# A drain on GpSimd behind each two-source operation of an attention, FFN and expert kernel

## Chip, cores and metric

One core of one Trainium2 chip runs the whole program in one launch. The metric is the device time of one execution in microseconds; the kernel before takes 838.08 us (median of 3 runs, 837.47 to 841.38).

## What is computed

The reference, cut to its three stages (all float32; B 4, H 8, S 576, head 64, model width 512, 8 experts):

```
proj = x @ w_phi; proj -= max(abs(proj)); phi = [exp(proj), exp(-proj)]      # of q and of k
attn = (phi(q) @ (phi(k).T @ v)) / (phi(q) @ sum(phi(k)) + 1e-6)
u    = x + (x.T @ U @ V).T                # x: the attention output, 512 wide
y    = u + relu(u @ w_ch1) @ w_ch2        # hidden width 2048
e    = argmax(y @ w_gate), or the token before's where sigmoid(y @ w_local) >= 0.5
out  = softmax(y @ w_gate)[e] * (relu(y @ w1[e]) @ w2[e])
```

## The kernel before

TensorE multiplies float32 as sums of rounded parts: every operand is split into a high part (rounded to the matmul's float32 form) and a low part (the rest), and each product takes three matmuls (`three`, L973 to L975, and `mm2`, L1075 to L1077). Products of the hidden layer go through a seven-product scheme on 2x2 blocks, so sums and differences of blocks have to be made ahead of the matmuls. All of this preparation is elementwise work:

- ScalarE copies a tile into its high part (L342, L514).
- VectorE or GpSimd subtracts it to get the low part (`both`, called in `w_end`, L336 on VectorE and L67 on GpSimd; `x_end`, L517).
- VectorE or GpSimd makes the sums and differences of blocks (`sums`, L336 and L67; `add` in `x_make`, L541).
- `narrow` (L77 to L90) turns 64-bit weights into 32-bit ones in six VectorE steps and a last addition on GpSimd (L67).
- In the expert stage GpSimd scales the finished output rows (`mm2`, L1095; the last two are VectorE's).

`in_halves` (L67) issues a 512-wide operation on GpSimd as two instructions of 256 columns.

The program has an attention stage (0 to about 228 us), four FFN units of four batches (items 0 to 15) and eight expert items (16 to 23), each of some 180 matmuls. The recording itself decides the order: `gate` and `either` hold a running estimate of when each engine will be free and give a preparation step to VectorE or GpSimd when it fits beside TensorE. The engines then run their instructions in that fixed order and wait on semaphores.

Evictions of matmul results read PSUM and at most one SBUF tensor: `u`, `y` and sums in PSUM (L946), `hlo` (L948). They stand in VectorE's queue behind the preparation steps. From item 12 on, `route` (L1110 to L1207) picks the expert of a batch with many tiny VectorE steps (128x5 and 128x40), among them `r_sm` plus 1e-9 (L1161), the sum of the softmax; GpSimd's queue then issues two small transfers (L1192 and L1193). GpSimd's queue also issues the reloads of activations `x` from DRAM (L596) in the FFN units.

Of the kernel before, what the change touches and what calls it, by code (L numbers as in the profile page):

```python
# [12 lines left out]
ALU = mybir.AluOpType  # L13
# [9 lines left out]
CH = 288  # L23
# [14 lines left out]
def model(ctx, tc, kq, vx, wphi, ident, up, vp, wff, wg, wmoe1, wmoe2, rconst, outT):  # L38
    nc = tc.nc
# [12 lines left out]
    def f32(ap):  # L52
        return ap.bitcast(F32)
# [7 lines left out]
    rows = [tmp_p.tile([128, S], F32, name=f"row{n}") for n in range(NROW)]  # L61
    rawfree = [raw_p.tile([128, 1024], U32, name=f"raw{n}") for n in range(2)]

    def in_halves(eng, dst, a, b, n, op):

        for sl in (slice(0, n // 2), slice(n // 2, n)):
            eng.tensor_tensor(out=dst[:, sl], in0=a[:, sl], in1=b[:, sl], op=op)  # L67

    def narrow(dst, raw, p, n, a=None, fine=False):

# [84 lines left out]
    def cost(eng, n):  # L155
        return {"DVE": (0.075 + n / 960) * 1.15, "ACT": 0.17 + n / 1330, "POOL": 0.05 + n / 340}[eng]
# [12 lines left out]
    def gate(eng, dur, *keys):  # L169

        if not late:
            yield "step"
        while late and not force[0]:
            at = max([free[eng]] + [touched.get(id(k), 0.0) for k in keys])
            if at + (0.0 if eng == "POOL" else dur) <= free["PE"] + SLACK[eng][at_step[0]]:
                break
            yield "wait"
        emitted[0] += 1
        force[0] = False
        if late:  # L180
            book(eng, dur, *keys)

    def either(eng, n, *keys):

        if not late:
            yield "step"
            emitted[0] += 1
            return eng
        while True:
            best = None  # L190
            for e, name, bias in ((nc.gpsimd, "POOL", 0.0), (nc.vector, "DVE", BIAS)):
                dur = cost(name, n)
                at = max([free[name]] + [touched.get(id(k), 0.0) for k in keys])
                ok = at + (0.0 if name == "POOL" else dur) <= free["PE"] + SLACK[name][at_step[0]]
                if (ok or force[0]) and (best is None or at + dur + bias < best[0]):
                    best = (at + dur + bias, e, name, dur)
            if best is not None:
                break
            yield "wait"
        emitted[0] += 1  # L200
        force[0] = False
        book(best[2], best[3], *keys)
        return best[1]
# [46 lines left out]
    def later(on, issue):  # L250

        if late:
            waiting.append((touched.get(id(on), 0.0), issue))
        else:
            issue()
# [8 lines left out]
    def take(free_):  # L264

        while not free_:
            yield "blocked"
        return free_.pop(0)
# [240 lines left out]
    def x_end(key, s, r, eng, own=None, then=None):  # L509

        x = xo[key][s] = yield from take(xfree)
        keys = (x,) if own is None else (x, own)
        yield from gate("ACT", cost("ACT", 2 * CH), *keys)
        nc.scalar.copy(out=x[:, 0], in_=r)  # L514
        for k in range(2):
            use = yield from either(eng, CH, *keys)
            use.tensor_tensor(out=x[:, 1, k], in0=r[:, k], in1=f32(x[:, 0, k]), op=ALU.subtract)  # L517
        if key in xd and s in XS:
            later(x, lambda: nc.sync.dma_start(out=f32(xd[key][XS.index(s)]), in_=f32(x)))
        xdone.add((key, s))  # L520
        if then is not None:
            then()

    def as_x(r):
        return r.rearrange("p (k t) -> p k t", k=2)

    def x_make(key, due=0, keep=True, plain=False, adds=nc.gpsimd, lows=nc.gpsimd):

        b = key[1]
        xo[key] = {}  # L530
        part = {f"B{k + 1}{t + 1}": y[:, 2 * k:2 * k + 2, b * S + t * CH:b * S + (t + 1) * CH] for k in range(2) for t in range(2)}
        if keep:
            xd[key] = dram.tile([7, 128, 2, 2, CH], F32R, name=f"xd{b}")

        def add(a, c, of_=None):
            r = yield from take(rows)
            x = as_x(r)
            keys = (r,) if of_ is None else (r, of_)
            for k in range(2):
                use = yield from either(adds, CH, *keys)  # L540
                use.tensor_tensor(out=x[:, k], in0=a[:, k], in1=c[:, k], op=ALU.subtract)  # L541
            return r

        def own(s):
            if late:
                spawn("x", due, x_end(key, s, part[s], lows))
            else:
                yield from x_end(key, s, part[s], lows)

        def made(s, r, last_=True):  # L550

            def then():
                if last_:
                    rows.append(r)

            if late:
                spawn("x", due, x_end(key, s, as_x(r), lows, r, then))
            else:
                yield from x_end(key, s, as_x(r), lows)
                if plain:  # L560
                    x_drop(key, s)
                    xdone.add((key, s))
                then()

        for s in ("B11", "B21", "B12", "B22") if plain else ("B11",):
            yield from own(s)
        t1 = yield from add(part["B12"], part["B11"])
        t2 = yield from add(part["B22"], as_x(t1), t1)
        yield from made("T2", t2, False)
        yield from made("T1", t1)  # L570
        while late and len([t for t in threads if t[2] == "x"]) > 2:
            yield "wait"
        t3 = yield from add(part["B22"], part["B12"])
        yield from made("T3", t3)
        while late and len([t for t in threads if t[2] == "x"]) > 2:
            yield "wait"
        t4 = yield from add(as_x(t2), part["B21"], t2)
        while (key, "T2") not in xdone:
            yield "wait"
        rows.append(t2)  # L580
        yield from made("T4", t4)
        if plain:
            xdone.difference_update([(key, s) for s in XS if s[0] == "T"])
        else:
            yield from own("B21")
            yield from own("B22")
# [320 lines left out]
    scale = {}  # L907
# [15 lines left out]
    def then(i):  # L923

        if i < 3:
            return x_make(("f", 3), 3, adds=nc.vector) if i == 1 else None
        to = i + 2 if i < 15 else i + 3
        if to < n and not held(i):
            key = x_key(to)
            return x_make(key, to, keep=False, adds=nc.vector) if key[0] == "m" else x_load(key)  # L930
        return None
# [130 lines left out]
    def mm2(i, t, d):  # L1062

        u, b = items[i]
        t0 = b * S + t * CH
        ps, m = bank()
        free["PE"] = max(free["PE"], ps_at[m])
        for k, f in enumerate((2, 3, 0, 1)):
            hhi, hlo = hh[t, f]
            w = need_w(u, f"V{f}")  # L1070
            free["PE"] = max(free["PE"], touched.get(id(w), 0.0))
            free["PE"] = max(free["PE"], hat[t, f])
            wh = w[:, 0, d * 128:(d + 1) * 128]
            wl = w[:, 1, d * 128:(d + 1) * 128]
            nc.tensor.matmul(ps, lhsT=wh, rhs=hhi, start=(k == 0), stop=False)  # L1075
            nc.tensor.matmul(ps, lhsT=wl, rhs=hhi, start=False, stop=False)  # L1076
            nc.tensor.matmul(ps, lhsT=wh, rhs=hlo, start=False, stop=(k == 3))  # L1077
            free["PE"] += 3 * MM
            touched[id(w)] = free["PE"]
        at = free["PE"] + SYNC  # L1080
        if last[u] == i and t == 1 and d == 3:
            for s in VS:
                wfree.append(u.w.pop(s))
        dst = y[:, d, t0:t0 + CH]
        yield

        if u.kind == "moe" and u.g == 0:
            ps_at[m] = act(lambda: nc.scalar.copy(out=dst, in_=ps), CH, at)
            return
        ps_at[m] = dve(CH, at, out=dst, in0=ps, in1=dst, op=ALU.add)  # L1090
        if u.kind == "moe":
            eng = nc.vector if i + 1 == n and t == 1 and d > 1 else nc.gpsimd
            free[of(eng)] = max(free[of(eng)], ps_at[m])
            book(of(eng), cost(of(eng), CH))
            eng.tensor_tensor(out=dst, in0=dst, in1=scale[u.b][:, t * CH:(t + 1) * CH], op=ALU.mult)  # L1095
            outs.append((outT[d * 128:(d + 1) * 128, t0:t0 + CH], dst))
            if t == 1 and d == 3:
                rows.append(scale[u.b])
            if i + 1 == n:
                store(0)  # L1100
# [255 lines left out]
    with tc.For_i(0, nl):  # L1356
# [34 lines left out]
        with tc.For_i(0, FT2) as j:  # L1391
# [3 lines left out]
            for c in range(2):  # L1395
                sl = slice(c * CH, (c + 1) * CH)
# [10 lines left out]
        dst = y[:, :, bass.ds(bv * S, S)]  # L1407
# [81 lines left out]
```

## Time and profile before

| | |
|---|---|
| median of the runs | 838.08 us |
| the profiled execution | 836.82 us, span 835.0 us |
| TensorE matmul busy | 772.0 us, 92% |
| VectorE busy | 616.4 us, 74% |
| GpSimd busy | 390.0 us, 47% |
| ScalarE busy | 330.3 us, 40% |
| mean granted TensorE clock | 0.965 |

An instruction's duration runs from its start to its end and holds any time that it spends blocked inside the engine; "idle before" is time in which the engine had nothing running. A GpSimd instruction that follows another without a pause starts some hundredths of a microsecond before the end of the one ahead.

### The profile page before, as it was taken

Reading aid. Unit: us, or ns where it says so; the run is one execution under the profiler, and the core shown is the slowest. Engines: PE = TensorE matmul, PEld = TensorE weight load, DVE = VectorE, ACT = ScalarE, POOL = GpSimd, SP = SyncE. Lnnn points to the kernel's source line nnn. Section 1 sums busy time; section 2 is a strip of 40 time slices with the busy share of each in tenths; the row PEclk is TensorE's granted clock in tenths of the full one; section 3 lists DMA queues with packets and bytes.
Section 4 is the critical chain, followed back from the end, with each engine's and each line's share of the span. In section 5 each row is a group of like instructions: output and inputs, shape, how many; then the busy total and the mean of one; then the engine's idle time right before and its main releaser. Section 6 shows DMA issues by size and latency. Waiting matters only on the chain.

```text
span 835.0 us, 20754 instructions
## 1 busy us (share of the span) xinstructions
PE 772.0 (92%) x8364; PEld 748.9 (90%) x8364; DVE 616.4 (74%) x1234; ACT 330.3 (40%) x788; POOL 390.0 (47%) x519
## 2 busy tenths in 40 slices
PE   8999899988799999999999999996959949989996
PEld 6898798987699999999999999996958949989996
DVE  7898788868896566866878654569787996975743
ACT  5766677742441312122121310241626426445440
POOL 1123463545770326323562331255656866677652
PEclk9999999998999999999999999998979979999998
DMA  6444454435871056310762046403232243242511
GB/s 188 142 142 146 165 189 171 159 145 200 294 301 42 2 189 198 137 51 28 248 224 63 14 130 205 177 2 106 83 107 79 67 126 91 75 127 92 165 46 59
DMA packets 45506, 108.01 MB, mean 129 GB/s; under 512 B 5408, under 2 KB 18848, under 8 KB 45408
## 3 DMA queue, kind: packets, MB, share of 16 engines
q1 hardware_dynamic: 35648, 78.29, 27.5%
q0 software_dynamic: 6304, 24.92, 9.2%
q10 hardware_dynamic: 3456, 3.46, 1.2%
q8 instruction: 66, 1.08, 0.5%
q14 instruction: 32, 0.26, 0.1%
HBM read 77.67 MB, written 28.98 MB: 128 GB/s over the span
## 4 chain that ended last, share of the span: by engine, by line
PE 59%; DVE 16%; issue 4%; POOL 2%; ACT 2%; DMA 1%; SPq 0%; ACTq 0%; DVEq 0%; POOLq 0%
PE psf L1075 10%; PE psf L1077 10%; PE psf L1076 10%; PE psf L973 9%; PE psf L974 9%; PE psf L975 9%; DVE r_sm L1161 2%; DVE x L517 1%; DVE w L336 1%; DVE y L946 1%; DVE row L541 1%; DVE row L85 1%; DVE row L80 1%; DVE pg L698 1%; PE num L761 1%
## 5 line engine op out<-in xcount | busy, mean ns | idle before, releaser
L973 PE MATMUL psf<-x,w 128*128 128x288 f32 x676 | 204.5, 302 | 35.2 <-DVE u L946 35.2
L1075 PE MATMUL psf<-hhi,w 128*128 128x288 f32 x768 | 229.4, 299 | 1.0 <-DVE hlo L948 1.0
L1076 PE MATMUL psf<-hhi,w 128*128 128x288 f32 x768 | 227.4, 296 | 0.0
L1077 PE MATMUL psf<-hlo,w 128*128 128x288 f32 x768 | 226.6, 295 | 0.0
L975 PE MATMUL psf<-x,w 128*128 128x288 f32 x676 | 203.7, 301 | 2.1 <-DVE w L336 1.9
L974 PE MATMUL psf<-x,w 128*128 128x288 f32 x676 | 204.2, 302 | 0.0
L973 PEld LDWEIGHTS psf<-x,w 128*128 128x128 f32 x676 | 131.8, 195 | 36.9 <-DVE u L946 36.9
L1075 PEld LDWEIGHTS psf<-hhi,w 128*128 128x128 f32 x768 | 144.9, 189 | 3.4 <-DVE hlo L948 1.5
L1077 PEld LDWEIGHTS psf<-hlo,w 128*128 128x128 f32 x768 | 145.2, 189 | 0.0
L1076 PEld LDWEIGHTS psf<-hhi,w 128*128 128x128 f32 x768 | 145.0, 189 | 0.0
L67 POOL TENSOR_TENSOR row<-row,row 128x256 f32<-128x256 f32 x94 | 68.9, 756 | 150.0 <-DVE row L90 145.5
L975 PEld LDWEIGHTS psf<-x,w 128*128 128x128 f32 x676 | 131.7, 195 | 2.6 <-DVE w L336 2.1
L962 ACT ACTIVATE hhi<-psf 128x288 fp32r<-128x288 f32 x192 | 68.6, 419 | 164.2 <-DVE psf L946 158.8
L974 PEld LDWEIGHTS psf<-x,w 128*128 128x128 f32 x676 | 131.8, 195 | 0.0
L946 DVE TENSOR_TENSOR y<-psf,y 128x288 f32<-128x288 f32 x160 | 72.1, 452 | 60.4 <-PE psf L1077 59.3
L67 POOL TENSOR_TENSOR w<-row,w 128x256 fp32r<-128x256 f32 x98 | 75.7, 799 | 77.2 <-ACT w L342 62.3
L948 DVE SCALAR_TENSOR_TENSOR hlo<-psf,hhi 128x288 fp32r<-128x288 f32 x192 | 77.3, 451 | 28.6 <-ACT hhi L962 28.6
L946 DVE TENSOR_TENSOR u<-psf,p 128x288 f32<-128x288 f32 x92 | 40.8, 452 | 37.2 <-PE psf L975 36.9
L1027 ACT COPY p<-psf 128x288 f32<-128x288 f32 x46 | 17.9, 401 | 123.5 <-PE psf L975 120.1
L67 POOL TENSOR_TENSOR w<-raw,w 128x256 fp32r<-128x256 f32 x58 | 46.4, 828 | 22.1 <-ACT w L342 20.2
L596 POOL DMA_DIRECT2D x<-xd x42 | 22.9, 545 | 66.6 <-PE psf L975 66.6
L342 ACT CAST w<-row 128x512 fp32r<-128x512 f32 x60 | 36.5, 629 | 42.4 <-POOL row L67 27.1
(127 smaller groups left out, 1280.2 us busy)
## 6 DMA issues: line engine op xcount, KB each, us to landing
x<-xd POOLq DMA_DIRECT2D x42, 576.0 KB, 6.7
raw<-in_wff SPq DMA_DIRECT2D x32, 512.0 KB, 3.6
xd<-x SPq DMA_DIRECT2D x28, 576.0 KB, 3.8
raw<-in_wmoe SPq DMA_DIRECT2D x52, 256.0 KB, 2.8
kq<-in_kq SPq DMA_DIRECT2D x14, 576.0 KB, 4.8
vt<-in_vx SPq DMA_DIRECT2D x16, 325.0 KB, 4.9
ys<-y SPq DMA_DIRECT2D x16, 288.0 KB, 2.1
outT<-y ACTq DMA_DIRECT2D x23, 144.0 KB, 1.8
```

The lines of the kernel that those rows point to most:

```text
L67: eng.tensor_tensor(out=dst[:, sl], in0=a[:, sl], in1=b[:, sl], op=op)
L342: nc.scalar.copy(out=w[:, 0], in_=f[:, :512])
L596: nc.gpsimd.dma_start(out=x, in_=xd[key][m])
L946: nc.vector.tensor_tensor(**kw)
L948: nc.vector.scalar_tensor_tensor(op1=op1, **kw)
L962: at = act(lambda: nc.scalar.activation(out=hhi, in_=src, func=ACTF.Relu), CH, ready)
L973: nc.tensor.matmul(ps, lhsT=w[:, 0, c], rhs=x[:, 0, k], start=(first and k == 0), stop=False, skip_group_check=True)
L974: nc.tensor.matmul(ps, lhsT=w[:, 0, c], rhs=x[:, 1, k], start=False, stop=False, skip_group_check=True)
L975: nc.tensor.matmul(ps, lhsT=w[:, 1, c], rhs=x[:, 0, k], start=False, stop=(stop and k == 1), skip_group_check=True)
L1075: nc.tensor.matmul(ps, lhsT=wh, rhs=hhi, start=(k == 0), stop=False)
L1076: nc.tensor.matmul(ps, lhsT=wl, rhs=hhi, start=False, stop=False)
L1077: nc.tensor.matmul(ps, lhsT=wh, rhs=hlo, start=False, stop=(k == 3))
```

## The change

A helper `paused` issues the two-source operation and, if the engine is GpSimd, a `drain` behind it. Four places use it: `in_halves`, the low parts in `x_end`, the differences in `x_make`, and the scaling in `mm2`.

```diff
+    def paused(eng, **kw):
+
+        eng.tensor_tensor(**kw)
+        if eng is nc.gpsimd:
+            nc.gpsimd.drain()
+
     def in_halves(eng, dst, a, b, n, op):
...
-            eng.tensor_tensor(out=dst[:, sl], in0=a[:, sl], in1=b[:, sl], op=op)
+            paused(eng, out=dst[:, sl], in0=a[:, sl], in1=b[:, sl], op=op)
...
-            use.tensor_tensor(out=x[:, 1, k], in0=r[:, k], in1=f32(x[:, 0, k]), op=ALU.subtract)
+            paused(use, out=x[:, 1, k], in0=r[:, k], in1=f32(x[:, 0, k]), op=ALU.subtract)
...
-                use.tensor_tensor(out=x[:, k], in0=a[:, k], in1=c[:, k], op=ALU.subtract)
+                paused(use, out=x[:, k], in0=a[:, k], in1=c[:, k], op=ALU.subtract)
...
-            eng.tensor_tensor(out=dst, in0=dst, in1=scale[u.b][:, t * CH:(t + 1) * CH], op=ALU.mult)
+            paused(eng, out=dst, in0=dst, in1=scale[u.b][:, t * CH:(t + 1) * CH], op=ALU.mult)
```

The built program gains 453 drains, all in GpSimd's queue and none with a semaphore. The other instructions of all five engines, their order and their waits are the same as before (the change moves none; `cost` and `book` know nothing of the drains). GpSimd's transfers (L596, L1192, L1193) get no drain behind them.

## Rows read from the trace of the kernel before

**Rows 1.** The page, busy time, share of the span and instructions of each engine
```profile
PE 772.0 (92%) x8364; PEld 748.9 (90%) x8364; DVE 616.4 (74%) x1234; ACT 330.3 (40%) x788; POOL 390.0 (47%) x519
```

**Rows 2.** Waits by line: engine line, waited for; us in total, times, longest
```profile
PE psf L973 <- DVE u L946: 35.2, 6, 9.4
```

**Rows 3.** Timeline of PE: start, us, line, shapes, count, idle before and releaser
```profile
577.61 0.61 PE L973 MATMUL psf<-x,w 128*128 128x288 f32 x1 [6.79 <-DVE u L946]
...
615.25 0.61 PE L973 MATMUL psf<-x,w 128*128 128x288 f32 x1 [9.38 <-DVE u L946]
...
682.35 0.61 PE L973 MATMUL psf<-x,w 128*128 128x288 f32 x1 [8.69 <-DVE u L946]
```

**Rows 4.** Timeline of POOL and DVE ahead of the first of these waits
```profile
566.71 0.51 POOL L1193 DMA_DIRECT2D sall<-row  x1
567.23 1.58 POOL L541 TENSOR_TENSOR row<-y 128x288 f32<-128x288 f32 x2
...
574.80 1.53 POOL L541 TENSOR_TENSOR row<-row,y 128x288 f32<-128x288 f32 x2
...
567.24 9.12 DVE L1161 TENSOR_SCALAR r_sm<-r_sm 128x5 f32<-128x5 f32 x1
```

**Rows 5.** The same ahead of the second
```profile
604.64 0.50 POOL L1193 DMA_DIRECT2D sall<-row  x1
605.15 2.31 POOL L517 TENSOR_TENSOR x<-row,x 128x288 fp32r<-128x288 f32 x3
...
605.65 7.29 DVE L1161 TENSOR_SCALAR r_sm<-r_sm 128x5 f32<-128x5 f32 x1
```

**Rows 6.** The same ahead of the third
```profile
671.58 0.50 POOL L1193 DMA_DIRECT2D sall<-row  x1
672.09 0.82 POOL L1095 TENSOR_TENSOR y<-y,row 128x288 f32<-128x288 f32 x1
...
679.84 1.39 POOL L67 TENSOR_TENSOR raw<-raw,raw 128x256 f32<-128x256 f32 x2
...
671.57 10.36 DVE L517 TENSOR_TENSOR x<-row,x 128x288 fp32r<-128x288 f32 x2
```

**Rows 7.** Timeline of DVE in the FFN stage, behind reloads on POOL
```profile
335.48 4.01 DVE L77 TENSOR_SCALAR row<-raw 128x512 uint32<-128x512 uint32 x1
```

**Rows 8.** Timeline of POOL and DVE, a run with no transfer ahead of it
```profile
598.96 3.29 POOL L67 TENSOR_TENSOR w<-raw,w 128x256 fp32r<-128x256 f32 x4 [4.35 <-ACT w L342]
...
600.38 1.26 DVE L336 TENSOR_TENSOR w<-raw,w 128x512 fp32r<-128x512 f32 x1
```

**Rows 9.** PE alone in stretches behind the waits: window, us, PE busy (x), PEclk, DMA
```profile
577.60:581.40 3.80, 3.79 (x16) 0.50 0.39 128
...
615.25:619.00 3.75, 3.75 (x16) 0.51 0.84 239
...
682.35:687.20 4.85, 4.85 (x20) 0.50 0.31 100
```

**Rows 10.** Lines L1478 and L1484 (count, min/median/max ns) and timeline of POOL
```profile
L1478 POOLq DRAIN  x1: 182/182/182, 0.3 to 0.3; - x1
...
0.75 0.35 POOL L750 MEMSET x<- 128x128 f32 x2 [0.29 <-POOLq L1478]
...
L1484 POOLq DRAIN  x3: 40/107/2434, 831.7 to 834.7; - x3
```

**Rows 11.** Stages: window, us, busy (x) of PE, PEld, DVE, ACT, POOL, PEclk, DMA
```profile
566.00:691.00 125.00, 96.45 (x683) 93.51 (x682) 106.06 (x199) 51.53 (x119) 79.70 (x103) 0.88 0.29 93
691.00:835.00 144.00, 134.53 (x998) 133.59 (x996) 90.76 (x174) 60.63 (x138) 89.33 (x107) 0.97 0.30 95
```

**Rows 12.** The chain that ended last, in order of time: start, us, what
```profile
152.31 2.28 POOL row L541 x3
...
647.68 2.43 POOL w L67 x3
...
654.44 1.41 POOL w L67 x2
```

## The prediction

> **What bounds the kernel now.** I read the page first: TensorE is busy for 772 of 835 us [rows 1], so what can be won lies in its idle time, not in GpSimd's 47%. The list of waits says who ends that idle time: one pair leads, a first matmul of a block product that waits for VectorE's eviction `u`, 35.2 us in only six waits, the longest 9.4 [rows 2]. Few and long means single events, so I went to the timeline of TensorE and found three that matter: 6.79, 9.38 and 8.69 us [rows 3], together 24.86 us.
>
> Next I looked at what VectorE did just ahead of each. Ahead of the first it spent 9.12 us in one addition on 128x5 numbers [rows 4]; ahead of the second 7.29 us in the same line [rows 5]; ahead of the third 10.36 us in two subtractions of 288 columns [rows 6]. Such sizes explain tenths of a microsecond. What stands beside each is the same: GpSimd has just issued its two small transfers and then runs one two-source operation after another without a pause, from 567.23 to 576.33 us, from 605.15 on, from 672.09 to 681.23 us. VectorE's instruction ends when that run ends: 567.24 + 9.12 = 576.36. All the blocked instructions take their inputs from SBUF and none from PSUM. I read this as GpSimd holding something in SBUF access that VectorE needs, and not letting go between its instructions.
>
> Two more rows narrow it. A run without a transfer ahead of it lets VectorE in: a subtraction that starts at 600.38 in the middle of four GpSimd operations takes 1.26 us, about one GpSimd operation of waiting and its own 0.6 [rows 8]. And behind reloads of `x`, also issued by GpSimd, a conversion step is again held for 4.01 us [rows 7]; there are two such blocks, and TensorE waits after neither. So five long blocks, each in an unbroken run behind a GpSimd transfer. A pause of GpSimd ends the block.
>
> The Trainium skill (GPSIMD Engine Reference, Instruction dispatch) says that a GpSimd core starts the next instruction when its own share of the last is done, without waiting for the other cores. That would fit cores that a transfer has put out of step, so that at no moment all have let go; no row here shows single cores.
>
> **The change, part by part.** It removes nothing and moves nothing; it adds 453 drains to GpSimd's queue. A drain there makes the next instruction wait until the one ahead has finished (the first one of [rows 10] lasts past the end of the memset ahead of it), so an unbroken run becomes operations with a pause between. I work out what that frees, then what it costs.
>
> *First stall.* The addition starts at 567.24 with GpSimd's first operation, whose spacing is 1.58/2 = 0.79. With a pause it goes in at about 568.1 instead of 576.36. From its end to TensorE's restart it took 577.61 - 576.36 = 1.25; one more step on that way reads two SBUF tensors and may wait for one more operation, 0.8. That makes 568.1 + 1.25 + 0.8 = 570.2, and TensorE ran dry at 577.61 - 6.79 = 570.82. The stall goes whole: 6.8 us. Behind it TensorE ran 3.80 us at a granted clock of 0.50, which is 1.2 GHz, for 16 matmuls [rows 9]; at 2.4 GHz half of that, 1.9, would do. Gain 8.7.
>
> *Second stall.* The addition goes in at 605.15 + 2.31/3 = 605.9. From its end (612.94) to TensorE's restart (615.25) it took 2.3, with three steps on the way that read two SBUF tensors, each of which may meet one GpSimd operation: between 0 and 3 x 0.8 more, I take 1.2. Restart at 609.4, where TensorE ran dry at 605.87: 3.5 us of stall stay, 5.9 go. I give the clock nothing back, since a stall stays; all of its 1.9 is the other bound.
>
> *Third stall.* The first subtraction goes in when the scaling behind the transfer ends, 672.91; the second meets one operation of 0.7. Each takes about 0.45 and the eviction another 0.45, so TensorE restarts near 672.9 + 0.45 + 0.7 + 0.45 + 0.45 = 675.0; it ran dry at 673.66. 7.3 of 8.69 go. The low clock behind it (4.85 us) I leave, with 2.4 as the other bound.
>
> Freed: 8.7 + 5.9 + 7.3 = 21.9 us. With everything freed it is 24.86 + 1.9 + 1.9 + 2.4 = 31.1.
>
> *The price of a drain.* The trace has no drain behind a two-source operation. At the start of the program one takes 182 ns while a memset finishes, and the whole pause that it, two semaphore steps and the start of the other engines make is 0.29 [rows 10]; that bounds it from above for a working queue. From below it is nothing. At the end of the program three drains take 0.04, 0.11 and 2.43 us on an idle engine; the last belongs to the closing of the program, and I keep it for a rival. I take 0.15, half of the nearest row, and 0.04 for the head start that operations in a run have today: 0.19 each.
>
> Most of that lies beside other work: GpSimd is idle for more than half of the span [rows 1]. On the path lie the GpSimd operations of the chain: 11 in a row from 647.68 to 655.85, and the stretch with three at 152.31, some 7 with their neighbours [rows 12]. 18 x 0.19 = 3.4 us. VectorE's conversion steps and evictions elsewhere I cost at nothing: those that read one SBUF tensor and PSUM are not held by GpSimd, and the others already wait for the operation in progress.
>
> Sum: 836.82 - 21.9 + 3.4 = 818.3 for the profiled execution. It stands 1.3 below the median of the runs, so I forecast **820**.
>
> **Rivals.**
>
> *GpSimd falls behind (faster, but less).* In the stage of the three stalls GpSimd is busy for 79.7 of 125 us [rows 11]. Without the stalls the stage is about 103 long, and some 97 operations with 0.19 each bring GpSimd to 98. It then has hardly slack, and weights and sums that are today ready in time come late; TensorE waits for them. If half of the added 18 us shows, 9 instead of 2, the time is 827. For it: the figures above. Against: in that stage GpSimd itself waits for 45 us.
>
> *The drain frees nothing (no change).* If the next GpSimd operation takes its hold again before VectorE's request is served, blocks stay and only the cost is left: 838.08 + 3.4 = 841, or 838 at a price of nothing. Against it: VectorE's instruction ended within 0.03 us of the end of the run [rows 4], so a short pause is enough. The Trainium skill (SBUF — State Buffer, SBUF: two separate sides) says that the side which starts first gets the shared ports for one whole instruction. By that rule VectorE's turn comes at the next instruction's end with or without a drain, the blocks would be something else, and this rival holds. Rows 8 agree with it; rows 4 to 6, where a whole run passes first, do not.
>
> *The drain is dear (slower).* From what price does it decide? The stage of the stalls has 103 - 79.7 = 23 us of slack for 97 drains, 0.24 each; the stage behind it 144 - 89.3 = 55 for 106, 0.52 each [rows 11]. Beyond that every 0.1 us costs some 10 us in the first alone. At 0.5 the gain is spent: 97 x 0.26 = 25 against 21.9. At 0.6 it is 838 - 22 + 97 x 0.36 + 106 x 0.08 + 3 = 862; at the 2.43 of rows 10 it would be several hundred more. For it: that one row. Against it: its two neighbours and the row at the start.
>
> **How the numbers follow.** The forecast, stalls freed and GpSimd in time, takes 0.66 and spans 806 (all 31.1 freed and drains for nothing: 838.08 - 31.1 = 807, less a microsecond) to 826. The first rival has 0.14 (826 to 834), the second 0.11, the third 0.09. A measurement of this kernel can tell 0.5%, 4.2 us, from no change: 833.9 to 842.3. Forecast and first rival lie below, so faster is 0.80, same 0.11, slower 0.09. The range of 806 to 834 holds the first two cases.
>
> **What would show it.** Right: line L1161 at 1 us or less in all four executions and no L517 of VectorE above some 1.5 us; the three waits of [rows 3] at 0, about 3.5 and 1.4 us; six waits of 35.2 us [rows 2] down to some 15; GpSimd's runs with pauses of 0.1 to 0.2 us, and its chain share somewhat up. Wrong: one L1161 still of several microseconds (the drain frees nothing); pauses of 0.5 us and more, or new TensorE waits released by GpSimd lines L67 and L517 (it falls behind).

## The result and the profile after

The change makes the kernel a little slower. The median is 842.22 us (839.21 to 845.39, 13 runs) against 837.53 us (833.38 to 841.38, 13 runs) for the kernel before: a ratio of 1.0056, with an interval of 1.0035 to 1.0076. The profiled execution took 839.38 us, its span 837.2. Forecast were 820 us and a range of 806 to 834. One run of the kernel before (1068.25 us) and one of an experiment's kernel (1880.12 us) were far slower than all others and count in no ratio below.

In the changed kernel the lines have moved by six (L1161 is L1167 now, L946 is L952, L973 is L979, L596 is L602), and every two-source operation that the change touched is recorded under the helper's line, L66, its drain under L68.

The page's line on busy time, to be read beside [rows 1]:

```profile
PE 776.4 (93%) x8364; PEld 749.5 (90%) x8364; DVE 583.9 (70%) x1234; ACT 329.8 (39%) x788; POOL 398.1 (48%) x519
```

VectorE is busy 32.5 us less for the same 1234 instructions: that is about what its five long blocks took. TensorE is busy 4.4 us more. Lines of VectorE that were blocked, in the view by source line (count, shortest/median/longest in ns, first and last start):

```profile
L1167 DVE TENSOR_SCALAR r_sm<-r_sm x4: 171/470/853, 550.7 to 644.9; 128x5 f32<-128x5 f32 x4
...
L83 DVE TENSOR_SCALAR row<-raw x34: 226/417/939, 17.5 to 490.8; 128x512 uint32<-128x512 uint32 x32, 128x160 uint32<-128x160 uint32 x1, 128x144 uint32<-128x144 uint32 x1
...
L66 DVE TENSOR_TENSOR x<-row,x x18: 440/678/1068, 226.4 to 735.0; 128x288 fp32r<-128x288 f32 x18
```

The addition that took 9.12 and 7.29 us [rows 4, 5] takes at most 0.85, the conversion step of 4.01 us [rows 7] at most 0.94, and the subtraction of the third block [rows 6] at most 1.07. So the drains do what they should: all five long blocks are gone. The waits of TensorE by pair, the largest total first, and its wait at the matmul of the second stall:

```profile
PE psf L979 <- DVE u L952: 16.9, 8, 4.1
PE psf L1081 <- DVE hlo L954: 6.3, 7, 1.7
...
PE psf L981 <- DVE w L342: 3.1, 2, 2.9
PE psf L979 <- ACT w L348: 3.0, 2, 2.4
PE psf L1082 <- POOL w L66: 1.9, 2, 1.3
...
614.96 0.41 PE L979 MATMUL psf<-x,w 128*128 128x288 f32 x1 [1.08 <-DVE u L952]
```

The pair that led with 35.2 us in six waits [rows 2] now has 16.9 in eight; at the matmuls of the three stalls of 6.79, 9.38 and 8.69 us [rows 3] TensorE now waits 0, 1.08 and 0 us. In their place stand many small waits that the kernel before hardly had. Where they come from shows in the waits of GpSimd and in the drains themselves:

```profile
POOL row L66 <- issue: 57.3, 49, 6.7
...
L68 POOLq DRAIN  x453: 424/846/7804, 19.3 to 829.6; - x151
```

A drain lies beside the operation ahead of it, so its median of 0.846 us is that operation's own length. But the longest lasts 7.80 us, and GpSimd stands 57.3 us in front of `row` operations where nothing that the profile shows holds it ("issue"). The timeline of GpSimd in the FFN stage shows one such place, the view of its drains there gives the drain's length, the view of the three reloads the time from issue to landing, and the view of DMA the packets of GpSimd's own queue, q0 (packets, MB, share):

```profile
349.11 1.63 POOL L602 DMA_DIRECT2D x<-xd  x3 [0.59 <-issue]
350.74 0.78 POOL L66 TENSOR_TENSOR row<-row,row 128x256 f32<-128x256 f32 x1
356.98 0.74 POOL L66 TENSOR_TENSOR row<-row,row 128x256 f32<-128x256 f32 x1 [5.47 <-issue]
357.88 1.60 POOL L66 TENSOR_TENSOR w<-row,w 128x256 fp32r<-128x256 f32 x2 [0.16 <-issue]
...
L68 POOLq DRAIN  x1: 6790/6790/6790, 350.1 to 350.1; - x1
...
DMA to landing us min/median/max: 4.3/5.2/6.5
...
q0 software_dynamic: 432, 1.77, 73.7%
...
359.21 0.40 PE L979 MATMUL psf<-x,w 128*128 128x288 f32 x1 [1.44 <-DVE u L952]
```

GpSimd issues three reloads of `x` and one operation, done at 351.52. The drain behind it holds until 350.1 + 6.79 = 356.89, and only then the next operation starts. The row of q0 is that of the window 349 to 356.2, in which the three reloads move their 1.77 MB; from 356.25 on that view has no row of q0. The drain ends 0.7 us after the last packet of the reloads. The third reload is issued at 350.2 and lands 6.5 us later, at 356.7, some 0.2 us ahead of the drain's end. The last row is TensorE's: 2.2 us after GpSimd goes on it waits 1.44 us at a matmul where it did not wait before.

The same behind the two small transfers, where a long block was before:

```profile
579.15 0.54 POOL L1198 DMA_DIRECT2D mine<-row  x1 [7.82 <-DVE r_fr L1161]
579.68 0.51 POOL L1199 DMA_DIRECT2D sall<-row  x1
580.20 0.82 POOL L66 TENSOR_TENSOR row<-y 128x288 f32<-128x288 f32 x1
583.29 0.81 POOL L66 TENSOR_TENSOR row<-y 128x288 f32<-128x288 f32 x1 [2.27 <-issue]
584.26 0.81 POOL L66 TENSOR_TENSOR row<-y,row 128x288 f32<-128x288 f32 x1 [0.16 <-POOL row L66]
```

The first operation runs 580.20 to 581.02, the second starts at 583.29. From there on the pauses are 0.16 to 0.23 us. Of the 453 drains, 15 are stretched like this, to between 2.8 and 7.8 us, all behind transfers that GpSimd issued; each ends 0.5 to 1.2 us after the last packet of q0, and 14 of them 0.1 to 0.2 us after the landing of the last transfer ahead (the other 0.6). Two more drains, of 1.8 and 1.9 us, have no transfer near them.

Where the time went by stage: of before first, then of the change (window, us, busy and instructions of PE, PEld, DVE, ACT, POOL, granted clock, DMA). The stages are cut at TensorE's restarts after the attention and where it ran dry ahead of the first of [rows 3], or at the like place.

```profile
0.00:228.30 228.30, 204.16 (x4157) 186.93 (x4157) 190.02 (x346) 138.17 (x337) 95.41 (x134) 0.97 0.51 176
228.30:570.80 342.50, 341.63 (x2567) 339.44 (x2567) 234.19 (x524) 81.79 (x200) 130.19 (x183) 0.99 0.37 126
570.80:835.00 264.20, 226.18 (x1642) 222.53 (x1641) 192.19 (x366) 110.35 (x252) 164.42 (x204) 0.93 0.30 93
```

```profile
0.00:233.10 233.10, 205.35 (x4156) 187.86 (x4156) 192.58 (x346) 138.13 (x337) 95.00 (x134) 0.97 0.51 172
233.10:588.50 355.40, 348.12 (x2603) 344.79 (x2603) 225.13 (x538) 82.46 (x201) 135.02 (x185) 0.99 0.37 125
588.50:837.20 248.70, 222.89 (x1606) 216.82 (x1605) 166.22 (x352) 109.18 (x250) 168.12 (x202) 0.96 0.31 94
```

Attention is 4.8 us longer. The FFN stage is 12.9 longer, of which 36 matmuls that went over from the last stage make 36 x 348.12/2603 = 4.8; 8.1 are real, and TensorE's idle time in it grows from 0.9 to 7.3 us. The last stage, that of the experts, is 15.5 shorter, by the same correction 10.7. Together 4.8 + 8.1 - 10.7 = 2.2, the difference of the two spans. (All kernels here issue the same 8364 matmuls in the same order. The times of one and the same matmul in both traces give the same three numbers.) The prediction had 18.5 of gain in one place; there are 10.7, and two losses where it expected next to nothing.

How attention loses its part shows in events that both kernels have. TensorE's timeline of before, and then of the change:

```profile
136.37 0.55 PE L741 MATMUL tq<-id_sb,pg 128*128 128x128 f32 x3 [0.58 <-ACT eq L744]
...
203.84 0.58 PE L804 MATMUL utps<-vs,ts 128*128 128x256 f32 x1 [3.56 <-DVE ts L790]
...
228.29 0.61 PE L973 MATMUL psf<-x,w 128*128 128x288 f32 x1 [5.98 <-DVE u L946]
```

```profile
138.57 0.55 PE L747 MATMUL tq<-id_sb,pg 128*128 128x128 f32 x3 [0.58 <-ACT eq L750]
...
207.78 0.39 PE L810 MATMUL utps<-vs,ts 128*128 128x256 f32 x1 [3.91 <-DVE ts L796]
...
233.13 0.61 PE L979 MATMUL psf<-x,w 128*128 128x288 f32 x1 [4.10 <-DVE u L952]
```

The same events come 2.2, 3.9 and 4.8 us later: a steady drift, with no single stall. And the chain that ended last has a member of its own now, by engine:

```profile
PE 47%; DVE 10%; POOLq 10%; issue 8%; ACT 2%; POOL 2%; DMA 1%; SPq 0%; ACTq 0%; DVEq 0%
```

POOLq, GpSimd's queue, has 10% of the span, all of it on the drains' line; the operation that each drain waits for is in that share.

### The profile page after: what moved, and what is told of

Its sections match the earlier page's. It is cut to its first block, busy times and chain, and to the rows that moved or that the text cites. A ratio compares the mean times of both kernels' runs of the same rounds, so it can differ in the third digit from the quotient of the medians.

```text
span 837.2 us, 21207 instructions
## 1 busy us (share of the span) xinstructions
PE 776.4 (93%) x8364; PEld 749.5 (90%) x8364; DVE 583.9 (70%) x1234; ACT 329.8 (39%) x788; POOL 398.1 (48%) x519
## 3 DMA queue, kind: packets, MB, share of 16 engines
q8 instruction: 66, 1.08, 0.5%
## 4 chain that ended last, share of the span: by engine, by line
PE 47%; DVE 10%; POOLq 10%; issue 8%; ACT 2%; POOL 2%; DMA 1%; SPq 0%; ACTq 0%; DVEq 0%
POOLq L68 10%; PE psf L1081 8%; PE psf L1082 8%; PE psf L1083 8%; PE psf L979 7%; PE psf L981 7%; PE psf L980 7%; DVE x L66 1%; DVE row L91 1%; DVE row L86 1%; POOL x L602 1%; ACT row L1184 1%; DMA row<-wdS 1%; DVE psf L952 1%; DVE u L952 1%
## 5 line engine op out<-in xcount | busy, mean ns | idle before, releaser
L979 PE MATMUL psf<-x,w 128*128 128x288 f32 x676 | 204.5, 302 | 21.4 <-DVE u L952 16.9
L979 PEld LDWEIGHTS psf<-x,w 128*128 128x128 f32 x676 | 131.3, 194 | 24.5 <-DVE u L952 18.8
L66 POOL TENSOR_TENSOR row<-row,row 128x256 f32<-128x256 f32 x94 | 71.1, 756 | 161.8 <-DVE row L96 96.3
L952 DVE TENSOR_TENSOR y<-psf,y 128x288 f32<-128x288 f32 x160 | 72.0, 451 | 62.2 <-PE psf L1083 61.8
L66 POOL TENSOR_TENSOR w<-row,w 128x256 fp32r<-128x256 f32 x98 | 77.6, 792 | 66.0 <-ACT w L348 38.8
L952 DVE TENSOR_TENSOR u<-psf,p 128x288 f32<-128x288 f32 x92 | 40.6, 451 | 44.4 <-PE psf L981 36.3
L66 POOL TENSOR_TENSOR w<-raw,w 128x256 fp32r<-128x256 f32 x58 | 46.8, 807 | 17.9 <-ACT w L348 8.3
L703 DVE TENSOR_REDUCE mx<-pj 128x6 f32<-128x768 f32 (+2 forms) x49 | 45.8, 934 | 7.8 <-PE pj L700 7.8
```

The costliest lines, as they stand in the source:

```text
L66: eng.tensor_tensor(**kw)
L703: nc.vector.tensor_reduce(out=mx[:, :, sl], in_=ps[:, :, sl], axis=AX, op=ALU.max, apply_absolute_value=True)
L952: nc.vector.tensor_tensor(**kw)
L979: nc.tensor.matmul(ps, lhsT=w[:, 0, c], rhs=x[:, 0, k], start=(first and k == 0), stop=False, skip_group_check=True)
```

## The experiments

The theory after the result, theory A: the blocks come from GpSimd's transfers, the drains free them and are worth some 22 us, and what eats the gain is that a drain behind a transfer waits until it has landed. Its rivals: that the blocks have another cause than the transfer, and that the pauses alone, 453 of them, are the price. Where an expectation weighs a narrower question, it says which answers it sets against each other.

The first four share their runs of the kernel before (median 836.99 us).

**The small transfers from another queue.** Before, with no drains:

```diff
-        nc.gpsimd.dma_start(out=mine[b], in_=tp)
-        nc.gpsimd.dma_start(out=late["sall"][8 * b:8 * b + 8], in_=tp)
+        nc.sync.dma_start(out=mine[b], in_=tp)
+        nc.sync.dma_start(out=late["sall"][8 * b:8 * b + 8], in_=tp)
```

> The kernel before, with the two small transfers of the expert choice (lines L1192 and L1193) issued by SP instead of GpSimd; no drains. Theory A (a transfer on GpSimd's queue makes the unbroken run behind it keep VectorE out): the addition L1161 takes 1 us or less in all four executions, no subtraction L517 of VectorE above 1.5 us, the three waits of 6.8, 9.4 and 8.7 us shrink to under 4 us each, time 812 to 822. Rival B (any long unbroken run of GpSimd keeps VectorE out, the transfers are a coincidence): at least one of these instructions still takes over 3 us, time 830 to 840.

Measured: 814.45 us (811.88 to 814.74), ratio 0.9744 (0.9701 to 0.9786). Its two lines of VectorE, by source line, then GpSimd and VectorE at the third of the four additions:

```profile
L1161 DVE TENSOR_SCALAR r_sm<-r_sm x4: 171/172/240, 540.5 to 631.2; 128x5 f32<-128x5 f32 x4
...
L77 DVE TENSOR_SCALAR row<-raw x34: 223/418/4031, 17.6 to 480.6; 128x512 uint32<-128x512 uint32 x32, 128x160 uint32<-128x160 uint32 x1, 128x144 uint32<-128x144 uint32 x1
...
598.24 2.32 POOL L517 TENSOR_TENSOR x<-row,x 128x288 fp32r<-128x288 f32 x3
600.52 4.59 POOL L67 TENSOR_TENSOR w<-raw,w 128x256 fp32r<-128x256 f32 x6
...
600.35 0.24 DVE L1161 TENSOR_SCALAR r_sm<-r_sm 128x5 f32<-128x5 f32 x1
```

The addition never exceeds 0.24 us. Not every one of the four is a test: at the place of [rows 4] GpSimd's run now begins behind the addition. The one shown is: it runs inside nine operations of GpSimd without a pause and is let in. The conversion step behind the reloads, which still go through GpSimd, is blocked for 4.03 us as before. The first rival falls: where the transfer leaves GpSimd, the block goes, and only there. What the three stalls are worth is 836.99 - 814.45 = 22.5 us; the prediction had worked out 21.9.

**One drain instead of 453.** Before, with a drain behind the second small transfer only, four in all:

```diff
         nc.gpsimd.dma_start(out=late["sall"][8 * b:8 * b + 8], in_=tp)
+        nc.gpsimd.drain()
```

> The kernel before with four drains in all, one behind each second small transfer (L1193). Theory A: each of the four drains lasts some 3 us (until the transfer has landed), and the run behind it lets VectorE in, since the drain has put the engine back in step: L1161 at 1 us or less, time 815 to 826. Rival B: the run behind the drain is as unbroken as before and holds a VectorE instruction for over 3 us again, time 830 to 842.

Measured: 814.24 us (811.43 to 815.4), ratio 0.9742 (0.9699 to 0.9786). The drains by source line, GpSimd's timeline at the first, and two steps of VectorE in the run behind it:

```profile
L1194 POOLq DRAIN  x4: 2734/4115/5571, 566.6 to 657.6; - x4
...
566.67 0.51 POOL L1193 DMA_DIRECT2D sall<-row  x1
570.19 1.58 POOL L541 TENSOR_TENSOR row<-y 128x288 f32<-128x288 f32 x2 [3.01 <-issue]
571.73 1.57 POOL L541 TENSOR_TENSOR row<-y,row 128x288 f32<-128x288 f32 x2
...
570.30 0.72 DVE L1205 TENSOR_SCALAR r_po<-rc_sb,r_pf 1x8 f32<-1x8 f32 x1
575.07 1.05 DVE L541 TENSOR_TENSOR row<-y 128x288 f32<-128x288 f32 x1
```

Directly behind a transfer, these drains last 2.7 to 5.6 us. The additions themselves test nothing here, since all four run while GpSimd stands in the drain. But the run behind is unbroken, and VectorE's steps in it are let in within one operation of GpSimd (the longest hold in the rest of this trace's stage is 1.4 us). So no pause between the operations is needed, against the prediction's reading: one drain between the transfer and the run is enough. And four waits of this kind cost nothing in the median here.

**Drains in one stage at a time.** All of the change's drains, but by the stage in which they are issued; in the first of these kernels from item 13 of the order on (the experts, 221 drains):

```diff
+    item = [-1]
+    def paused(eng, **kw):
+        eng.tensor_tensor(**kw)
+        if eng is nc.gpsimd and item[0] > 12:
+            nc.gpsimd.drain()
...
+        item[0] = i
```

> The change with its drains from item 13 on alone (221 of 453). Theory C (the gain of the change lies in the expert stage, its loss ahead of it, and the two add): the stretch from the first long wait on is 15 us shorter as in the changed kernel, and nothing is lost ahead, time 818 to 826. Rival D (work that comes late in the expert stage eats the gain wherever the drains stand): 830 to 842.

Measured: 827.03 us (825.85 to 828.7), ratio 0.9895 (0.9863 to 0.9928), 10.0 us faster than before, between the ranges of theory C and rival D. It agrees with the 10.7 of the windows, and it is 12.8 us above the kernel with four drains: more than half of the gain is given back in the very stage that has it.

The next has `-1 < item[0] < 13` as its condition (the FFN stage, 128 drains):

> The change with its drains in items 0 to 12 alone (128 of 453), where GpSimd issues the reloads of x. Theory E (a drain behind a transfer of GpSimd lasts until the transfer has landed): some eleven drains of 3 to 8 us, the rest about 0.85 us, and a time 10 to 16 us above the kernel before, 848 to 854. Rival F (only the pause of some 0.16 us behind each operation costs): no drain over 1.5 us, time 838 to 842.

Measured: 845.43 us (841.57 to 850.65), ratio 1.0126 (1.007 to 1.0183): 8.4 us slower, a little less than expected, and the 8.1 of the windows. By source line, and TensorE's waits:

```profile
L70 POOLq DRAIN  x128: 510/836/8552, 213.7 to 498.9; - x128
...
PE psf L981 <- DVE u L954: 38.0, 10, 9.3
```

Ten of these drains last 3.7 to 8.6 us.

The third has `item[0] < 0` (attention, 104 drains; runs of before with a median of 837.36 us, as for the three that follow it):

> The change with its drains in the attention stage alone (104 of 453), where GpSimd issues no transfer. Theory G (the pause behind each operation, 0.14 to 0.16 us and the lost head start, lies on the path here, since VectorE and GpSimd hand work to each other): no drain over 1.5 us but for waits of the operation ahead, first FFN matmul stage some 5 us later, 841 to 845. Rival H (the pause is hidden, and the changed kernel's late start has to do with the transfers behind it): 835 to 839.

Measured: 841.12 us (835.5 to 845.0, 12 runs), ratio 1.0049 (1.0018 to 1.008): 3.8 us slower. No drain of these is over 1.35 us: GpSimd issues no transfer in that stage, so this is the price of the pauses alone (1.5 to 6.7 us by the interval). The three stages sum to -10.0 + 8.4 + 3.8 = 2.2 us; the change itself measured 4.7 (842.22 - 837.53).

**Only the drains behind reloads.** Before, with one drain behind the first two-source operation after each group of reloads of the FFN stage, ten in all:

```diff
+        eng.tensor_tensor(**kw)
+        if eng is nc.gpsimd and reloaded[0]:
+            nc.gpsimd.drain()
+            reloaded[0] = False
...
+            reloaded[0] = item[0] < 13
```

> The kernel before with ten drains in all, each behind the first two-source operation that follows a reload of x in the FFN items. Theory E (what the FFN items lose is the wait for the landing of the reloads): ten drains of 3 to 8 us, and most of the 8 us that 128 drains cost there, 842 to 847. Rival F (it is the pause behind every operation): the ten drains cost next to nothing on the path, 836 to 840.

Measured: 845.14 us (836.0 to 848.24), ratio 1.0108 (1.0054 to 1.0161), the drains 3.96 to 9.09 us long. Ten drains lose 7.8 us, within the spread as much as the stage's 128, so the other 118 seem free. Its profiled execution happened to be the fastest of the six, 836.0: in it the FFN stage is 3.7 us longer, matmul by matmul, and the stretch of the three stalls behind it as much shorter.

**The price in the experts' stage without the small transfers.** The small transfers on SP as in the first experiment, and the 221 drains:

> The small transfers on SP, and the change's drains from item 13 on (221): none of these has a transfer of GpSimd to wait for, but those behind the last reload. Theory G (the pause behind each operation costs on the path): 822 to 828, some 8 to 13 us above the 814.4 of the same kernel without drains, with new TensorE waits released by lines of GpSimd. Rival I (the landing of the small transfers was the cost there): 813 to 818.

Measured: 818.04 us (817.03 to 819.05), ratio 0.9786 (0.9742 to 0.9831). It lies at the upper edge of rival I's range, below theory G's. Against its own runs of before it gains 837.36 - 818.04 = 19.3 us, where the same kernel without drains gained 22.5: the pauses, with the landing of the seven reloads that are left on GpSimd in this stage, cost 3.2, which is within the noise of two such differences. The same drains with the small transfers on GpSimd gained 10.0: 9.3 us hang on the landing of four pairs of small transfers, which alone, with four drains, cost nothing.

The traces show where, one execution of each kernel. The first stretch runs from the start of the last matmul ahead of the first of [rows 3] to that of the matmul of the third, the second from there to the end (us):

| kernel | first stretch | second stretch |
|---|---|---|
| before | 111.8 | 152.7 |
| small transfers on SP, no drain | 89.6 | 149.4 |
| four drains, directly behind the transfers | 92.5 | 149.5 |
| small transfers on SP, 221 drains (this one) | 89.9 | 154.4 |
| transfers on GpSimd, 221 drains | 98.9 | 155.3 |

In the first stretch the pauses alone cost 0.4 us, the four waits alone 2.9, and both together 9.3: the two costs don't add. In the second, when all small transfers have been issued, the pauses cost 5.0. The chain of the changed kernel, in order of time, shows one such place:

```profile
613.55 0.45 POOL mine L1198
...
615.39 2.48 issue
617.86 0.83 POOLq L68
...
624.48 0.45 PE psf L1082
```

From the transfer at 613.55 on, the chain goes through the wait behind it (2.48 us) and seven operations with a pause behind each, to a matmul at 624.48 that waits 1.25 us for a weight tile. At the same matmul neither the kernel with four drains nor this one waits. So it looks as if the pauses use up the slack that covered the waits.

**No transfer on GpSimd at all.** Before without drains, the reloads on SP too:

```diff
-            nc.gpsimd.dma_start(out=x, in_=xd[key][m])
+            nc.sync.dma_start(out=f32(x), in_=f32(xd[key][m]))
```

> The kernel before with all 50 transfers of GpSimd's queue (reloads of x and the small ones) issued by SP, no drains. Theory A: the two blocks of 4 us of line L77 in the FFN items are gone as well, no VectorE instruction held over some 2 us by GpSimd. Rival B: they stay. Time: 812 to 818 if SP's queue takes the reloads without keeping weight loads waiting behind them; more if it does.

Measured: 810.63 us (807.65 to 813.68), ratio 0.9699 (0.9651 to 0.9746). It is the fastest kernel of this study and beats both. By source line, and TensorE's leading wait:

```profile
L77 DVE TENSOR_SCALAR row<-raw x34: 225/418/1059, 16.4 to 477.8; 128x512 uint32<-128x512 uint32 x32, 128x160 uint32<-128x160 uint32 x1, 128x144 uint32<-128x144 uint32 x1
...
PE psf L973 <- DVE u L946: 14.5, 4, 6.8
```

The blocks behind the reloads are gone as well, without one drain, and in this trace no instruction of VectorE lasts over 0.7 us longer than the shortest of its shape, less than one operation of GpSimd.

**All 453 drains, no transfer on GpSimd.** Runs of before with a median of 838.08 us, for this one and the next:

> The change with all its 453 drains, and all 50 transfers of GpSimd's queue issued by SP, so that no drain has a transfer to wait for. Theory E plus G (the loss of the change was the landing of transfers, and besides a pause of some 0.16 us per operation): no drain over 2 us; time 810.6 without drains plus some 4 in the attention stage and 4 in the expert stage, 816 to 822. Rival J (the drains cost the same wherever the transfers are): 830 to 840.

Measured: 822.42 us (816.58 to 828.09), ratio 0.9822 (0.9787 to 0.9856).

```profile
L68 POOLq DRAIN  x453: 422/844/1894, 18.3 to 807.5; - x151
```

The longest drain falls from 7.80 us to 1.89. Against the kernel without drains, each by its own runs of before, the pauses cost (837.36 - 810.63) - (838.08 - 822.42) = 11.1 us. This kernel's runs spread widely, so the number is good to some 5 us; the parts found above, 3.8 in attention and 5.4 in the traces of the experts' stage, come to 9.2.

**The FFN stage's 128 drains, no transfer on GpSimd.** This is the pair to the kernel that lost 8.4 us:

> All 50 transfers on SP, and the 128 drains of items 0 to 12 alone. Theory E (what these drains cost in the kernel with GpSimd's transfers, 8 us, was the landing of the reloads): 809 to 813, the same as without drains. Rival F (the pause behind each operation): 816 to 822.

Measured: 811.76 us (810.83 to 812.75), ratio 0.9684 (0.9667 to 0.9702), which cannot be told from the kernel without drains. By source line, and the stage in the view of windows:

```profile
L70 POOLq DRAIN  x128: 549/839/1909, 215.5 to 487.9; - x128
...
230.60:566.00 335.40, 334.52 (x2516) 332.55 (x2517) 220.41 (x510) 79.85 (x196) 107.94 (x138) 0.99 0.35 126
```

The same 128 drains at the same places, and TensorE is idle for 335.40 - 334.52 = 0.9 us in the stage, as before the change. The second rival falls as the whole explanation: in this stage the pauses cost nothing, and the whole loss is the wait for the landing. In attention (3.8 us) and with the experts they do have a price.

## Why the prediction was wrong

**What it had right.** The three stalls, that VectorE is blocked behind GpSimd's transfers, and their worth: 21.9 worked out, 22.5 and 22.8 measured in the two kernels that free them alone. The rows it named came as it said: L1161 at 0.85 us at most, 0, 1.08 and 0 us left of the three stalls, the pair of 35.2 us at 16.9. The price of a drain behind an operation, "0.15, half of the nearest row, and 0.04 for the head start", was nearly right too: the pause is 0.14 to 0.16 in most places and 0.20 to 0.25 in a fifth of them.

**The step that failed.** The price of a drain: "A drain there makes the next instruction wait until the one ahead has finished", which made each of the 453 cost 0.19 us, wherever it stands. The sign against it was in the rows: "At the end of the program three drains take 0.04, 0.11 and 2.43 us on an idle engine; the last belongs to the closing of the program, and I keep it for a rival." The row of 2.43 us [rows 10] showed that a drain can last long on an idle engine, and it was set aside as a rival of 0.09, thought of as a price for each drain. No run shows what that one waited for. But for the change the right question was what else than an operation a drain waits for, and the prediction had named the candidate itself: reloads and small transfers on the same queue. A drain behind one of them lasts until it has landed, 2.7 to 9.1 us.

**What hung on it.** The FFN stage was costed at nothing. It was asked who waits for VectorE there, but not who waits for GpSimd behind the ten places with reloads: 8.4 us. In the experts' stage the same waits, on top of the pauses, gave back 12.8 of 22.8 us. The forecast also looked at the stage's slack for one cost alone: in the stretch of the three stalls it is enough for the pauses (0.4), nearly enough for the four waits (2.9 in the traces, nothing in the medians), not for both (9.3).

**A term that was mis-sized.** The pauses on the path were put at 18 x 0.19 = 3.4 us; all 453 without transfers cost 11.1, some 3.8 of it in attention, where the prediction counted seven operations. The chain shows the operations of one execution's last path; the drift of 4.8 us must come in part from operations beside it, though no run names them.

The sum with what was measured: 837.5 - 22.8 (stalls) + 11.1 (pauses) = 825.8, which lies in the range. The change took 842.2; the 16.4 between are, within the noise, the landing waits: 8.4 measured in the FFN stage and 9.3 in that of the experts, 17.7 together.

**The rivals.** "GpSimd falls behind" is what happened in the stage of the experts, but there the pauses did it only together with the waits for landings. "The drain is dear" had the right sign and the wrong form: not each drain is dear, but 15 of 453. "The drain frees nothing" fell with the first rows. The Trainium skill (SBUF — State Buffer, SBUF: two separate sides) has the shared port pair held for one whole instruction. The trace without transfers on GpSimd agrees (VectorE held for 0.7 us at most, less than one operation of GpSimd). The traces behind a transfer do not: VectorE was kept out for 9.12 us [rows 4], one operation after another.

**What stays open.** Why a transfer issued by GpSimd leaves it in a state that keeps VectorE out until a drain or the end of the run. By the Trainium skill (GPSIMD Engine Reference, Instruction dispatch) a GpSimd core starts the next instruction when its own share of the last is done. Cores that are out of step would fit, also with one drain as the cure; no run here shows single cores. Nor does a run separate the landing from work of GpSimd's own on the transfer that ends with it: with the transfers on SP both are gone. That nearly every drain behind a transfer ends 0.1 to 0.2 us behind the landing speaks for the landing.

## What to carry to other kernels

Before adding a drain (or any wait for an engine to be idle), look at which transfers that engine has issued ahead of it: here a drain leaves a pause of some 0.16 us behind an operation and lasts up to 9.1 behind a DMA. Where a block stands behind transfers of one queue, try first to issue them from another; that gave 837.4 to 810.6 us with three lines, while the 453 drains gave a loss. And a stage's slack covers a cost only once: the pauses (0.4 us) and the waits (2.9) that were nearly free alone cost 9.3 together.

## What the runs showed of the hardware

- A drain on GpSimd waits for the transfers that GpSimd issued ahead of it, and ends 0.4 to 1.4 us after their last packet, mostly 0.1 to 0.2 us after the landing: 2.7 to 9.1 us, against 0.85 us in the median (the operation itself). With the transfers on SP the longest of the same 453 drains went from 7.80 to 1.89 us.
- VectorE's instructions with SBUF inputs can stay blocked for 4 to 10 us when GpSimd runs operations without a pause behind a DMA that it issued. With one drain between, or the DMA from SP, an unbroken run lets them in: the steps shown in such runs took 0.24 to 1.05 us.
- The pause that a drain leaves between two operations of GpSimd was 0.14 to 0.16 us in most places, 0.20 to 0.25 in a fifth.
